# A two-level Strassen kernel for attention and four experts: seeding one product's PSUM bank from another, the second level for one more chunk, and a planner that takes what is due first

## The chip, the cores and the metric

One core of a Trainium2 chip runs the whole program. The metric is device time in microseconds (us) of one execution. Three executions of the kernel before took 1754.56, 1755.11 and 1755.19 us, so the median is 1755.11 us.

## What is computed

All data are float32. The first half is an attention without softmax, in 8 batches of 8 heads, 576 rows, 64 columns a head. Its result is laid out as 4608 tokens by 512 columns. The second half runs every token through 4 experts and adds the results with weights.

```python
kv  = einsum('bhsd,bhse->bhde', k, v)
out = einsum('bhsd,bhde->bhse', q, kv)
x   = out / sqrt(mean(out * out, -1) + 1e-6) * g_norm     # then (4608, 512)
p   = domain_probs / (domain_probs.sum(-1) + 1e-9)
for e in range(4):
    h    = maximum(x @ w1[e], 0)       # w1[e]: 512 x 1024
    out += p[:, e:e+1] * (h @ w2[e])   # w2[e]: 1024 x 512
```

## The kernel before

**Tiling.** The 4608 tokens are cut into 9 chunks of 512: chunk c of 0 to 7 has the first 512 rows of batch c, chunk 8 has the 64 rows left of each batch. For each expert e and each chunk c there is a step s = 9e + c, 36 in all, with an "up" part (x times w1) and a "down" part (h times w2). The step's down part runs beside the up part of the next step.

**Products.** Matrix products are done with Strassen's scheme (seven block products in place of eight, at the price of sums of blocks). `up` (L779) uses it twice: an outer loop over seven blocks m, and within each an inner loop over seven products mm in the order `ORDER = (1, 2, 6, 5, 7, 4, 3)` (L381), so 49 products a step. Each is two matmuls with 128 moving columns (L809). Only the first step is done plainly (`up_plain`, L878). The down part has two forms. `down` (L999) uses one level: seven products in two halves of tokens, each of four matmuls with 256 moving columns (L1017), 56 matmuls a step. `down_deep` (L1038) uses two levels: the seven outer blocks go in four groups, (1, 6), (7, 5), (4, 2) and (3), and for each group the seven inner products are made of 4 matmuls (2 in the last group) with 128 moving columns (L1090), 98 matmuls a step. The profile counts two records for each of these float32 matmuls. L1212 selects: `down_deep` for experts 1 to 3 and chunks 1 to 6, `down` for the rest.

**What an inner round does.** TensorE (PE) accumulates products 1, 6, 7, 4 of a round one after another in one PSUM bank (`u1` in `up`, `db` in `down_deep`), and the running sum is taken out after each by ScalarE (ACT): after 1, 6 and 7 into a buffer called `snap`, after 4 into its place in the result (L825, L1115). Product 2 has a bank of its own (`u2`, `ab`), and products 5 and 3 share a third. VectorE (DVE) adds a bank and a snap into the result (`total`, L833 and L1123): bank of 2 plus snap 1, bank of 5 plus snap 7, bank of 5 and 3 plus snap 6. There are two slots for each of the kinds `u1`, `u2`, `db` and `ab`[...]. In `up` the seven results are then added up (`combine`, L339, on DVE or on GpSimd, POOL), and a Relu on ACT (L792) gives h.

**What sets the order.** Nothing is ordered by hand. The class `Plan` (L34) holds every operation with a key (its place in the work), the engines that may do it and a cost. `layout` (L77) then walks through time: each free engine looks at its operations in order of key, up to a reach of 0.7 to 1.0 steps ahead, and takes the first one that is ready (its predecessors' ends plus 0.3 us across engines, 0.06 us on one), gives it its slots, and goes on. The result is a fixed order on each engine. A `port` operation on POOL also waits for the last such operation on DVE (L1234). Weights of the next expert are loaded during chunk 8 of the one before (L1201). The last step's result is written by SyncE (SP) with plain DMAs (L989), those of experts 1 to 3 otherwise by POOL with adding DMAs (L987).

Of the kernel before, what the change touches and what calls it, by code (L numbers as in the profile page):

```python
# [24 lines left out]
class Op:  # L25
    def __init__(self, key, cost, fn, reads, writes, kb, port):
        self.key, self.cost, self.fn, self.kb, self.port = key, cost, fn, kb, port
        self.outs = list(writes)
        self.bufs = list(dict.fromkeys(list(reads) + self.outs))
        self.deps = {}  # L30
        self.start = self.end = self.eng = None


class Plan:  # L34


# [9 lines left out]

    SPARE = {"big": 6, "small": 3}

    def __init__(self):
# [27 lines left out]
    def layout(self, slots, later, idle, idle_banks, idle_until):  # L77
# [14 lines left out]
        for e in todo:  # L92
            todo[e].sort(key=lambda o: (o.key, o.n))
        busy = {e: 0.0 for e in todo}
        bus = port = 0.0
# [27 lines left out]
        while left:  # L123
# [4 lines left out]
            for eng in todo:  # L128
# [5 lines left out]
                if not pending:  # L134
                    continue
                reach = pending[0].key + self.REACH[eng]
                for op in pending:
                    if op.key > reach:
                        break
                    if op.start is not None:  # L140
                        continue
                    when = ready(op, eng)
                    if when is None:
                        continue
                    if when > t:
                        heapq.heappush(wake, when)
                        continue
                    op.start, op.eng = t, eng
                    if eng == "SP":
# [35 lines left out]
                    moved = True  # L185
                    break
                if eng == "PE" and busy[eng] <= t and 1.6 <= t and front < idle_until:
# [26 lines left out]
def kernel(  # L214
# [9 lines left out]
    out: bass.AP,  # L224
):


# [152 lines left out]

    ORDER = (1, 2, 6, 5, 7, 4, 3)  # L381
    MERGED = (1, 6, 5, 7, 4, 3, 2)
# [396 lines left out]
    def up(s, e, views):  # L779
# [16 lines left out]
        for i, m in enumerate(OUTER):  # L796
            n = f"{s}_{m}"
            whole = made[m] = Buf("big", f"m{n}")
            bank = {1: Buf("u1", f"u1_{n}"), 2: Buf("u2", f"u2_{n}")}
            snap = {}  # L800
            for j, mm in enumerate(ORDER):
                key = s + (i + j / 7) / 7
                if mm == 5:
                    bank[2] = Buf("u2", f"u3_{n}")
                ps = bank[1 if mm in (1, 6, 7, 4) else 2]

                def product(eng, m=m, mm=mm, ps=ps):
                    for u in range(2):
                        nc.tensor.matmul(  # L809
                            ps.ap[:, u * P:(u + 1) * P],  # L810
                            lhsT=w1f[e][m][mm][1]()[:, u * P:(u + 1) * P], rhs=views[m][mm][1](),
                            start=(mm in (1, 2, 5) and u == 0), stop=True, skip_group_check=True,
                        )

                op = plan.add(
                    key, pe(2, P), product, reads=w1f[e][m][mm][0] + [views[m][mm][0]], writes=[ps],
                    after=last[-2:-1] if mm in (1, 2) else (),
                )
                if mm == 3:
                    last.append(op)  # L820

                def copy(to, where, ps=ps, key=key):
                    plan.add(
                        key - 0.4, act(HN),
                        lambda eng: nc.scalar.activation(  # L825
                            out=where(), in_=ps.ap[:, 0:HN], func=ACT.Copy),
                        reads=[ps], parts=[to],
                    )
# [8 lines left out]

                if mm in (1, 6, 7):
                    snap[mm] = Buf("snap", f"s{mm}_{n}")
                    copy(snap[mm], lambda b=snap[mm]: b.ap[:])  # L840
                if mm == 2:
                    total(0, 0, ps, snap[1])
                elif mm == 7:
                    total(1, 1, bank[2], snap[7])
                elif mm == 4:
                    copy(whole, lambda whole=whole: block(whole, 1, 0))
                elif mm == 3:
                    total(0, 1, ps, snap[6])
# [29 lines left out]
    def up_plain(s, e, c, key, span):  # L878
# [4 lines left out]
        for i in range(8):  # L883
            uh, a, u = i // 4, i // 2 % 2, i % 2
            bank = Buf("u1" if a == 0 else "u2", f"up{s}_{i}")
            for dh in range(2):
                w, low = corners[uh, dh]

                def product(eng, w=w, bank=bank, dh=dh, ut=2 * a + u):
# [6 lines left out]

                plan.add(
                    key + span * i / 8 - (1.1 if i < 4 and dh == 0 else 0.0), pe(2, NT), product,
                    reads=[w, low, xh[dh]], **({"parts": [bank]} if dh else {"writes": [bank]}),
                )  # L900
            for th, n in enumerate((1, 21) if uh == 0 else (2, 4)):
                plan.add(
# [96 lines left out]
    def down(s, e, c):  # L999
# [4 lines left out]
        for t in range(2):  # L1004
            banks = {}
            for j, m in enumerate(MERGED):
# [8 lines left out]
                def product(eng, m=m, t=t, ps=ps):  # L1015
# [10 lines left out]
                    after=second[-1:] if t and m in (1, 5) else (),  # L1026
                )
                if m == 2:
                    second.append(op)
# [8 lines left out]
    def down_deep(s, e, c):  # L1038
# [8 lines left out]
        for i, group in enumerate(((1, 6), (7, 5), (4, 2), (3,))):  # L1047
# [28 lines left out]
            outs = [pair] + [half[m] for m in group]  # L1076
            bank = {1: Buf("db", f"d1_{s}_{i}"), 2: Buf("ab", f"d2_{s}_{i}")}
            snap = {}
            for j, mm in enumerate(ORDER):
                key = at + n * j / 49  # L1080
                if mm == 5:
                    bank[2] = Buf("ab", f"d3_{s}_{i}")
                ps = bank[1 if mm in (1, 6, 7, 4) else 2]

                def product(eng, group=group, mm=mm, ps=ps, forms=forms):
                    for o, m in enumerate(group):
                        b, at = forms[m][mm]
                        for kt in range(2):
                            col = at * HN + kt * P
                            nc.tensor.matmul(  # L1090
                                ps.ap[:, o * P:(o + 1) * P], lhsT=b.ap[:, col:col + P],
                                rhs=w2q[e][m][mm][1]()[:, kt, :],
                                start=(mm in (1, 2, 5) and o == 0 and kt == 0), stop=(kt == 1),
                                skip_group_check=True,
                            )

                op = plan.add(
                    key, pe(2 * n, P), product,
                    reads=[b for m in group for b in (w2q[e][m][mm][0], forms[m][mm][0])],
                    writes=[ps], after=inner_last[-2:-1] if mm in (1, 2) else (),  # L1100
                )
                if mm == 3:
                    inner_last.append(op)
# [8 lines left out]
                def copy(where, key=key, ps=ps, n=n, group_of=group_of, **kw):  # L1112
                    plan.add(
                        key - 0.4, act(n * P),
# [14 lines left out]

                if mm in (1, 6, 7):  # L1130
                    snap[mm] = Buf("snap", f"ds{mm}_{s}_{i}")
                    copy(lambda b=snap[mm], g=group_of: g(b.ap), parts=[snap[mm]])
                if mm == 2:
                    total(0, 0, ps, snap[1])
                elif mm == 7:
                    total(1, 1, bank[2], snap[7])
                elif mm == 4:
# [57 lines left out]
    for e in range(E):  # L1195
        for c in range(NCH):
# [13 lines left out]
            if c == 1 and e:  # L1210
                inner[e]()
            if e and 1 <= c < NCH - 2:  # L1212
                down_deep(s, e, c)
# [9 lines left out]
    with tc.manual_schedule(engines={ENG.PE, ENG.DVE, ENG.Activation, ENG.Pool, ENG.SP}):  # L1223
# [4 lines left out]
        nc.vector.memset(bd_home[:], 0.0)  # L1228
        held = None
        for op in order:  # L1230
            made = op.fn(op.eng)
            if op.port and op.eng == "DVE":
# [33 lines left out]
```

## Time and profile before

The profiled execution took 1754.1 us; its span from the first to the last instruction is 1752.3 us, so 1.8 us lie around it. It is 1.0 us below the median of the three timed ones.

| engine | busy us | share of the span | instructions |
|---|---|---|---|
| PE, matmul | 1744.0 | 100% | 13970 |
| PE, weight load | 1659.0 | 95% | 13970 |
| DVE | 1119.1 | 64% | 1904 |
| POOL | 826.0 | 47% | 793 |
| ACT | 808.8 | 46% | 1897 |

PE's granted clock is 1.000. "Busy" for PE is a union of modelled, overlapping intervals: the mean of a matmul record (275 ns at 128 columns) is from its start to its modelled end, and the next starts long before that. What a matmul takes from PE is the distance between starts. A row such as `x8` in the timeline has eight records, and its first start and the next row's start give that distance.

### The profile page before, as it was taken

How to read it: one execution, taken by the hardware profiler on the slowest of the kernel's cores; microseconds unless marked ns; L12 is line 12 of the kernel's file. 1: busy time of each engine (PE TensorE's matmuls, PEld its weight loads, DVE VectorE, ACT ScalarE, POOL GpSimd, SP SyncE). 2: the span in 40 equal slices, each digit the busy share in tenths (PEclk: the TensorE clock that was granted, in tenths of full speed). 3: DMA queues.
4: the chain of work that ended last, by engine and by line, in shares of the span. 5: the costliest groups of instructions: out<-in, count | busy, mean ns of one | idle time of the engine just before them, and what ended most of it. 6: DMA issues, size and time to landing. Idle time of an engine off the chain costs nothing.

```text
span 1752.3 us, 35867 instructions
## 1 busy us (share of the span) xinstructions
PE 1744.0 (100%) x13970; PEld 1659.0 (95%) x13970; DVE 1119.1 (64%) x1904; ACT 808.8 (46%) x1897; POOL 826.0 (47%) x793
## 2 busy tenths in 40 slices
PE   9999999999999999999999999999999999999998
PEld 7799999999999999999999999999999999999997
DVE  4755554455674677777674577777674577777654
ACT  3454544454333445555543345555543445555541
POOL 2644553554345434444455534444455634444520
PEclk9999999999999999999999999999999999999999
DMA  9755544442443334444555434444465434444441
GB/s 236 242 160 161 167 128 136 151 140 85 148 153 103 106 100 110 109 109 109 136 154 133 108 95 110 108 111 107 111 169 136 117 98 108 111 108 111 109 109 37
DMA packets 148587, 220.78 MB, mean 126 GB/s; under 512 B 49601, under 2 KB 90817, under 8 KB 148417
## 3 DMA queue, kind: packets, MB, share of 16 engines
q1 hardware_dynamic: 133312, 191.21, 34.8%
q0 software_dynamic: 15104, 27.27, 11.0%
q8 instruction: 110, 1.80, 0.4%
q14 instruction: 61, 0.49, 0.1%
HBM read 145.30 MB, written 73.14 MB: 125 GB/s over the span
## 4 chain that ended last, share of the span: by engine, by line
PE 98%; SPq 1%; DMA 0%; POOL 0%; DVE 0%; issue 0%; ACT 0%
PE u L809 44%; PE db L1017 19%; PE db L1090 13%; PE ab L1090 10%; PE ab L1017 6%; PE u L891 2%; PE ab L602 1%; PE ab L584 1%; PE ab L612 1%; PE ab L569 1%; SPq L345 1%; DMA big<-in_v_dram 0%; PE ab L651 0%; POOL rt L521 0%; PE ab L666 0%; PE ab L636 0%
## 5 line engine op out<-in xcount | busy, mean ns | idle before, releaser
L833 DVE TENSOR_TENSOR big<-u,snap 128x256 f32<-128x256 f32 x696 | 290.6, 422 | 304.1 <-PE u L809 217.9
L809 PE MATMUL u<-xf,big 128*128 128x128 f32 x3248 | 453.9, 275 | 0.0
L825 ACT ACTIVATE snap<-u 128x256 f32<-128x256 f32 x735 | 281.7, 384 | 339.0 <-PE u L809 276.8
L339 DVE TENSOR_TENSOR big<-big,big 128x1024 f32<-128x1024 f32 (+1 forms) x354 | 410.6, 1175 | 32.9 <-ACT big L792 13.1
L809 PEld LDWEIGHTS u<-xf,big 128*128 128x128 f32 x3248 | 417.4, 192 | 7.3 <-issue 0.2
L809 PE MATMUL u<-xf,w1y 128*128 128x128 f32 x2652 | 371.6, 275 | 0.0
L809 PEld LDWEIGHTS u<-xf,w1y 128*128 128x128 f32 x2652 | 334.3, 192 | 2.0
L339 POOL TENSOR_TENSOR big<-big,big 128x256 f32<-128x256 f32 (+1 forms) x177 | 247.0, 1399 | 179.6 <-DVE big L339 67.2
L1017 PE MATMUL db<-big,big 128*128 128x256 f32 x1336 | 315.7, 380 | 0.0
L1017 PEld LDWEIGHTS db<-big,big 128*128 128x128 f32 x1336 | 241.6, 190 | 26.5
L792 ACT ACTIVATE big<-big 128x1024 f32<-128x1024 f32 x127 | 133.5, 1052 | 17.9 <-DVE big L339 12.4
L825 ACT ACTIVATE big<-u 128x256 f32<-128x256 f32 x232 | 89.0, 383 | 102.0 <-PE u L809 96.8
L987 POOL DMA_DIRECT2D out_dram<-big x110 | 100.3, 976 | 71.6 <-ACT big L964 53.0
L1115 ACT ACTIVATE snap<-db 128x256 f32<-128x256 f32 x216 | 76.6, 355 | 111.6 <-PE db L1090 100.8
L1123 DVE TENSOR_TENSOR big<-ab,snap 128x256 f32<-128x256 f32 (+1 forms) x204 | 79.0, 387 | 63.3 <-PE ab L1090 39.7
L339 POOL TENSOR_TENSOR big<-big 128x512 f32<-128x512 f32 (+1 forms) x75 | 89.6, 1200 | 63.0 <-DVE big L339 36.6
L964 ACT ACTIVATE big<-db,p_all 128x256 f32<-128x256 f32 x104 | 49.3, 474 | 141.0 <-PE db L1017 141.0
L1151 POOL TENSOR_TENSOR big<-big 128x512 f32<-128x512 f32 x19 | 24.1, 1269 | 164.4 <-DVE big L339 164.4
L971 DVE SCALAR_TENSOR_TENSOR big<-db,p_all,big 128x256 f32<-128x256 f32 x85 | 41.1, 483 | 86.4 <-PE db L1017 85.9
L1090 PE MATMUL db<-big,big 128*128 128x128 f32 x688 | 95.6, 275 | 0.0
L1090 PEld LDWEIGHTS db<-big,big 128*128 128x128 f32 x688 | 86.2, 192 | 0.1
L1017 PE MATMUL ab<-big,big 128*128 128x256 f32 x344 | 80.5, 379 | 0.0
(192 smaller groups left out, 2508.8 us busy)
## 6 DMA issues: line engine op xcount, KB each, us to landing
xf<-x SPq DMA_DIRECT2D x108, 512.0 KB, 3.5
out_dram<-big POOLq DMA_DIRECT2D x94, 256.0 KB, 5.3
xf<-x_h SPq DMA_DIRECT2D x81, 256.0 KB, 3.1
xf<-x SPq DMA_DIRECT2D x81, 256.0 KB, 3.3
x<-xf SPq DMA_DIRECT2D x36, 512.0 KB, 3.9
big<-in_moe_w_dram SPq DMA_DIRECT2D x28, 512.0 KB, 4.9
small<-in_q_dram SPq DMA_DIRECT2D x72, 128.0 KB, 3.7
kv<-in_k_dram SPq DMA_DIRECT2D x30, 288.0 KB, 3.4
```

The lines of the kernel that those rows point to most:

```text
L339: lambda eng: adder(eng).tensor_tensor(out=out_(), in0=a(), in1=b(), op=op),
L792: lambda eng: nc.scalar.activation(out=b.ap[:], in_=b.ap[:], func=ACT.Relu),
L809: nc.tensor.matmul(ps.ap[:, u * P:(u + 1) * P], lhsT=w1f[e][m][mm][1]()[:, u * P:(u + 1) * P], rhs=views[m][mm][1](), start=(mm in (1, 2, ...
L825: lambda eng: nc.scalar.activation(out=where(), in_=ps.ap[:, 0:HN], func=ACT.Copy),
L833: lambda eng: nc.vector.tensor_tensor(out=block(whole, a, t), in0=src.ap[:, 0:HN], in1=add_.ap[:], op=ALU.add),
L964: lambda eng: nc.scalar.activation(out=cell(i, half), in_=ap(), func=ACT.Copy, scale=prob()),
L971: lambda eng: nc.vector.scalar_tensor_tensor(out=cell(i, half), in0=ap(), scalar=prob(), in1=cell(i, half), op0=ALU.mult, op1=ALU.add,),
L987: nc.gpsimd.dma_start(out=dst, in_=cell(i)[parts, :], accum_op=ALU.add)
L1017: nc.tensor.matmul(ps.ap[:, 0:HN], lhsT=four(h[m])[:, kt // 2, t, kt % 2, :], rhs=w2f[e][m].ap[:, kt * HN:(kt + 1) * HN], start=(m in (1, ...
L1090: nc.tensor.matmul(ps.ap[:, o * P:(o + 1) * P], lhsT=b.ap[:, col:col + P], rhs=w2q[e][m][mm][1]()[:, kt, :], start=(mm in (1, 2, 5) and o ...
L1115: lambda eng: nc.scalar.activation(out=where(), in_=group_of(ps.ap), func=ACT.Copy),
L1123: lambda eng: nc.vector.tensor_tensor(out=cell(tq, dq), in0=group_of(src.ap), in1=group_of(add_.ap), op=ALU.add,),
```

## The change

Three things are changed.

**The seed.** After product 1, ACT copies the bank not into a snap but into the bank of product 2, and product 2 is added on top of it by PE (`start` is no longer set for it; it works on `parts` of the bank and reads it). What ACT then copies out is the finished block (0, 0), so DVE's `total(0, 0, ...)` is gone and a copy by ACT is there instead. The order of inner products becomes (1, 6, 2, 5, 7, 4, 3). Products 5 and 3 have their own buffer from the start of the round, and product 5 has to come after the copy that seeds (`after=seeds`). In `down_deep` the third bank of the last group is of kind `db`. An assertion while instructions are written out demands that PE's last product in the same slot was at least as wide as the seed.

**The second level for chunk 7.** L1212 becomes `c < NCH - 1`: steps 16, 25 and 34 are now done by `down_deep`.

**What is due first.** Each operation gets a due time: its key times 44 us (20 us later if PE isn't one of its engines), lowered where an operation that needs it is due earlier. ACT, DVE and POOL now take, of the operations within reach that are ready, the one with the earliest due time, in place of the first in order of key. PE and SP still take the first.

```diff
+        for op in self.ops:
+            op.due = op.key * self.STEP + (0.0 if "PE" in op.cost else self.LATE)
+        for op in reversed(self.ops):
+            for d in op.deps:
+                cross = self.SAME if op.cost.keys() == d.cost.keys() else self.CROSS
+                d.due = min(d.due, op.due - cross - min(d.cost.values()))
...
+                    if best is not None and op.due >= best.due:
                         continue
                     when = ready(op, eng)
...
+                    best = op
+                    if eng in ("PE", "SP"):
+                        break
...
-    ORDER = (1, 2, 6, 5, 7, 4, 3)
+    ORDER = (1, 6, 2, 5, 7, 4, 3)
...
-            bank = {1: Buf("u1", f"u1_{n}"), 2: Buf("u2", f"u2_{n}")}
+            bank = {
+                1: Buf("u1", f"u1_{n}"), 2: Buf("u2", f"u2_{n}"), 5: Buf("u2", f"u3_{n}"),
+            }
...
-                            start=(mm in (1, 2, 5) and u == 0), stop=True, skip_group_check=True,
+                            start=(mm in (1, 5) and u == 0), stop=True, skip_group_check=True,
...
-                    key, pe(2, P), product, reads=w1f[e][m][mm][0] + [views[m][mm][0]], writes=[ps],
-                    after=last[-2:-1] if mm in (1, 2) else (),
-                )
+                    key, pe(2, P), product,
+                    reads=w1f[e][m][mm][0] + [views[m][mm][0]] + ([ps] if mm == 2 else []),
+                    **{"parts" if mm == 2 else "writes": [ps]},
+                    after=last[-2:-1] if mm == 1 else seeds if mm == 5 else (),
+                )
...
-                if mm in (1, 6, 7):
+                if mm == 1:
+                    seeds = [copy(bank[2], lambda b=bank[2]: b.ap[:, 0:HN])]
+                elif mm in (6, 7):
                     snap[mm] = Buf("snap", f"s{mm}_{n}")
                     copy(snap[mm], lambda b=snap[mm]: b.ap[:])
                 if mm == 2:
-                    total(0, 0, ps, snap[1])
+                    copy(whole, lambda whole=whole: block(whole, 0, 0))
                 elif mm == 7:
-                    total(1, 1, bank[2], snap[7])
+                    total(1, 1, bank[5], snap[7])
...
-            if e and 1 <= c < NCH - 2:
+            if e and 1 <= c < NCH - 1:
                 down_deep(s, e, c)
```

`down_deep` has the same edits as `up`.

## The prediction

> **What bounds the kernel.** I read the page's totals first, then the chain that ended last, then PE's timeline for gaps, then the chain's end.
>
> ```profile
> PE 1744.0 (100%) x13970; PEld 1659.0 (95%) x13970; DVE 1119.1 (64%) x1904; ACT 808.8 (46%) x1897; POOL 826.0 (47%) x793
> ...
> PE 98%; SPq 1%; DMA 0%; POOL 0%; DVE 0%; issue 0%; ACT 0%
> PE u L809 44%; PE db L1017 19%; PE db L1090 13%; PE ab L1090 10%; PE ab L1017 6%; PE u L891 2%; PE ab L602 1%; PE ab L584 1%; PE ab L612 1%; PE ab L569 1%; SPq L345 1%; DMA big<-in_v_dram 0%; PE ab L651 0%; POOL rt L521 0%; PE ab L666 0%; PE ab L636 0%
> ```
>
> The chain is PE almost throughout: L809 (up), L1017 (plain down), L1090 (deep down). No other engine is busy over 64%. PE's timeline says what a matmul record takes, from start to start:
>
> ```profile
> 683.05 1.06 PE L1090 MATMUL db<-big,big 128*128 128x128 f32 x8
> 683.94 0.61 PE L809 MATMUL u<-xf,big 128*128 128x128 f32 x4
> 684.39 0.61 PE L809 MATMUL u<-xf,w1y 128*128 128x128 f32 x4
> 684.84 0.61 PE L1090 MATMUL ab<-x_rem,big 128*128 128x128 f32 x4
> 685.28 0.61 PE L1090 MATMUL ab<-kv,big 128*128 128x128 f32 x4
> 685.73 0.61 PE L809 MATMUL u<-xf,w1y 128*128 128x128 f32 x4
> ...
> 1723.26 8.80 PE L1017 MATMUL db<-big,big 128*128 128x256 f32 x40
> ...
> 1735.35 8.80 PE L1017 MATMUL ab<-big,big 128*128 128x256 f32 x40
> ```
>
> 683.05 to 685.73 is 24 records of 128 columns in 2.68 us: 0.1117 each. 1723.26 to 1735.35 is 56 records of 256 columns (40, and two rows of 8 left out) in 12.09 us: 0.2159 each. With such distances for every kind of record I went along PE's whole timeline. After about 80 us there is no gap over 0.2 us, and after about 450 us none at all. Up to 80 us PE loses 5.4 us in seven places, 2.6 of them on the first load of q. So nothing in the steady part can be won by shortening a wait: only PE work taken away counts, or waits brought in.
>
> **Part 1: the second level for chunk 7.** Three steps lose 56 matmuls of 256 columns and get 98 of 128. The order of the changed program's instructions confirms the counts (L1017's matmuls 1008 to 840, L1090's 1764 to 2058). Two records a matmul: 336 x 0.2159 = 72.5 us go, 588 x 0.1117 = 65.7 us come. Minus 6.9 us, all on the path.
>
> A rule speaks against this. The Trainium skill, "TensorE: Matmul & The Clock Gate", section "Back-to-back issue gap", gives about 81 ns a matmul at N = 128 in a real stream where weight loads count too, and 109.2 ns at N = 256 for the isolated gap (N/2.4 + 2.5). By that ratio, 0.74, the small record would cost 0.160 us, the new work 94.1 us, and the edit would lose 21.6 us. Here the ratio in the trace is 0.1117/0.2159 = 0.52, within rows where every record has its weight load (13970 of each). The row decides.
>
> What comes with it off PE: per step the deep form adds 21 subtractions and 7 sums on DVE or POOL and replaces 14 merges out of PSUM by 8 out of SBUF. The order has 1710 operations on DVE for 1902 and 753 on POOL for 788, so both are relieved over the program; ACT has 2273 for 1896. The next expert's weights are loaded in just that stage, and the deep form holds `big` buffers longer. I looked from which PE product each load is freed to the first product that reads its tile: the tightest w1 load has 47 us of PE work in between, 49 before. Landing takes 4.9 us (median) and two or three sums of 1.4 to 2.4 us follow. Cost nothing; it would begin to cost only if 35 us were eaten.
>
> **Part 2: the seed.** PE's products stay. Per round ACT has five copies for four, DVE two sums for three: 245 rounds in `up`, 84 in `down_deep`. DVE sheds 245 x 0.422 = 103 us there, which nobody waits for. The copy into PSUM has no row before. The nearest is L825, bank to snap, 384 ns. The skill's "ScalarE: Activation LUTs", section "Step-by-step: what each stage is for", holds that ScalarE writes faster to PSUM than to SBUF. By the rule it lies below 384 and by the row at 384; upwards I bound it at twice the row, 0.77. I take 0.38, the row it is nearest to.
>
> On ACT's queue the new copy stands in front of the snaps and Relus, and PE's product 6 and then 2 wait for it. How long a hand-over takes is seen where PE stalled:
>
> ```profile
> 73.42 0.60 PE L612 MATMUL ab<-ident,small 128*128 128x128 f32 x4
> 74.80 0.66 PE L569 MATMUL ab<-ident,small 128*128 128x128 f32 x4 [0.78 <-ACT big L618]
> ```
> ```profile
> 74.06 0.69 ACT L618 ACTIVATE big<-ab,gcol 128x512 f32<-128x512 f32 x1
> ```
>
> Four transposes of 0.109 end at 73.86. ACT starts 0.20 later, ends at 74.75, and PE goes on 0.05 later. So a copy of 256 columns needs 0.20 + 0.38 + 0.05 = 0.63 us from product to product on one bank, one of 128 columns (275 ns) 0.53. In the changed order I summed PE's work between two products on one bank. In `up`, after the start, four places have 0.89 us and the other 966 have 1.29 or more; before it was one at 0.89, which did not stall. In `down_deep` fifteen have 0.89, all in the last group with the short copy. At 0.77 for a copy the need is 1.02: 4 x 0.13 = 0.5 us. So the seed costs 0 if ACT is free. ACT is not always free:
>
> ```profile
> 664.70:708.50 43.80, 43.80 (x394) 43.80 (x394) 31.83 (x57) 22.98 (x56) 21.83 (x21) 1.00 0.43 107
> ```
>
> (Columns: window, length, then busy us of PE, weight load, DVE, ACT, POOL.) ACT gets 7 x 0.384 + 3 x 0.381 + 0.275 = 4.1 us more in a step: 27.1 of 43.8, 62%. That leaves room; a Relu of 1.05 us in front of a copy makes 1.7 us, and can stall a place of 1.29 by 0.4. Before, such places existed in the same number (301 products that wait 1.3 us behind ACT, 288 after) and none stalled. I take 0, and 2 us as the upper end.
>
> **Part 3: what is due first.** It moves work on ACT, DVE and POOL only; what it costs shows at the two ends.
>
> At the start, product 6 now comes 0.39 us after product 1 (it was two products later): needs 0.63, costs 0.25. One transpose that stalled 0.5 us on DVE has one product less in front of it: up to 0.45 more. The three 1024-wide sums that DVE now does first (3 x 1.22 us) delay forms that lay ready by 30 us and are needed at about 60: free. I take +0.5, between -1.5 (most of the waits of 0.54, 0.94 and 0.50 us near 70 us go) and +1.5.
>
> At the end, the last down part needs h2, the last sum of `up`, and then h3. Before:
>
> ```profile
> 1720.65 0.42 DVE L833 TENSOR_TENSOR big<-u,snap 128x256 f32<-128x256 f32 x1
> 1720.98 2.35 DVE L339 TENSOR_TENSOR big<-big,big 128x1024 f32<-128x1024 f32 x2
> ...
> 1723.37 1.06 ACT L792 ACTIVATE big<-big 128x1024 f32<-128x1024 f32 x1 [1.16 <-DVE big L339]
> ...
> 1724.81 2.68 POOL L339 TENSOR_TENSOR big<-big,big 128x1024 f32<-128x1024 f32 x1
> ```
>
> h3 was ready at 1727.5; PE asked for it three products after 1723.26, at 1728.4. In the changed order h2 goes to POOL, behind a port wait on a DVE sum (L1151) of the deep step that now fills this stage. From the last product of `up`: 0.20 to DVE, 0.42 + 0.29 + 0.78 for three DVE operations, 0.38 to POOL (as ACT to POOL above), 2.5 (between the 2.37 of L339's mean and 2.68), 0.1 and 1.05 for Relu, 0.1 and 1.23 for h3 on DVE, 0.05: 7.1 us. PE has two deep pairs and three plain products until then: 0.45 + 0.45 + 3 x 1.727 = 6.1 us. A stall of 1.0, between 0.3 and 2. Two hand-overs with 0.45 us of cover (need 0.53) just ahead disappear in it. The last store keeps its place: eight DMAs after the last merge.
>
> **The sum.** -6.9 + 0 + 0.5 + 1.0 = -5.4 us. Against the profiled execution: 1754.1 - 5.4 = 1748.7. The median is 1.0 above that execution: 1749.7.
>
> **The rivals.**
>
> *More is won.* The new choice also clears the startup waits and the tail isn't late: -6.9 - 1.5 + 0.3 = -8.1, so 1747.0. For it: 2.0 us of startup waits are behind ACT or DVE. Against: the same pairs stand next to each other in the new order (the 0.94 wait has still no work in front of it).
>
> *The gain is largely given back.* ACT at 62% meets Relu and copy at once more often than before: 2 us in the middle, 2 at the end, 1.5 at the start. 1755.1 - 6.9 + 5.5 = 1753.7, no change that counts. Against: no stall in 1300 us before.
>
> *Slower: the seed is late.* PE stands for each seed until ACT has done it. With c the time of a copy, its time in the queue included, PE loses c + 0.25 less the work in front. Summed over the changed order's places: 0.7 + 3.1 us at c = 0.8, 1.5 + 6.3 at 1.0, 5.6 + 9.4 at 1.1. It decides from c of about 1.0, where it eats the 6.9; at 1.1 the time is 1755.1 - 5.4 + 15 = 1764.7. For it: ACT is in order, and DVE's sum waited for nothing of the kind. Against: c would have to be 2.6 times the nearest row.
>
> *It doesn't do what it says.* If PE overwrote the seed rather than adding, instructions and waits would be the same, and so the time: no case of its own.
>
> **Chances and range.** Forecast 1749.7: 0.67. More won: 0.13. Given back: 0.15. Slower: 0.05. A measurement of this kernel tells about 0.2%, 3.5 us, from no change. The first two are faster by more: 0.80; the third is the same: 0.15; the last slower: 0.05. The range goes from 1746.8, just past the second case, to 1753.2, short of the third's 1753.7, which has all three uncertain ends (start, middle, tail) at their worst at once. About 0.85 lies within.
>
> **What would show it.** Right: L1017 with 1680 records and the 128-column kinds with 588 more, at unchanged distances; no PE gap between 100 and 1690 us; a seed row on ACT near 0.38; one PE wait of about 1 us near the end, behind h3. Wrong: PE waits on ACT at products 6 or 2 in the middle; a seed row over 0.8; another distance of the 128-column records; PE waiting on weights near 900 or 1300 us.

## The result, and the profile after

The changed kernel takes 1748.39 us (median; 1746.86 to 1748.91) against 1754.84 for the kernel before (four executions by now): ratio 0.9962, 95% interval 0.9945 to 0.9979, 6.5 us less. The forecast was 1749.7. The profiled execution took 1748.91 us with a span of 1747.1, 5.2 less than the profiled one before, where 5.4 had been worked out. How close these two come is luck, as the stretches below show.

The page's totals, and its chain by engine:

```profile
PE 1738.6 (100%) x14222; PEld 1664.1 (95%) x14222; DVE 1151.4 (66%) x1712; ACT 931.6 (53%) x2274; POOL 719.7 (41%) x758
...
PE 99%; DMA 0%; DVE 0%; ACT 0%; SPq 0%; issue 0%; ACTq 0%
```

PE has 252 records more, 588 less 336, and yet ends earlier. ACT is busy 123 us longer, POOL 106 us less. DVE has 192 operations fewer and yet is busy 32 us longer, since it now does more of the wide sums that either engine may do (`combine`, 429 against 354 in the largest group). The chain is PE still. What a record costs is read from PE's timeline, as before:

```profile
682.97 0.61 PE L1119 MATMUL db<-big,small 128*128 128x128 f32 x4
683.41 1.06 PE L830 MATMUL u<-xf,big 128*128 128x128 f32 x8
684.31 0.61 PE L1119 MATMUL ab<-x_rem,big 128*128 128x128 f32 x4
684.75 0.61 PE L1119 MATMUL ab<-kv,big 128*128 128x128 f32 x4
685.20 0.61 PE L830 MATMUL u<-xf,big 128*128 128x128 f32 x4
685.65 1.06 PE L830 MATMUL u<-xf,w1y 128*128 128x128 f32 x8
686.54 0.61 PE L830 MATMUL u<-xf,big 128*128 128x128 f32 x4
...
1730.18 5.34 PE L1044 MATMUL ab<-big,big 128*128 128x256 f32 x24
1735.37 1.89 PE L1044 MATMUL ab<-big,small 128*128 128x256 f32 x8
1737.09 1.89 PE L1044 MATMUL ab<-small,big 128*128 128x256 f32 x8
1738.82 3.62 PE L1044 MATMUL ab<-big,big 128*128 128x256 f32 x16
```

(L830 is `up`, L1119 `down_deep`, L1044 `down`; before they were L809, L1090, L1017.) 682.97 to 686.54 is 32 records in 3.57 us: 0.1116 each. 1730.18 to 1738.82 is 40 in 8.64: 0.2160. The distances are those of before, so the exchange gives its 6.9 us in full.

For every kernel here I cut PE's time in two: its records times their distances ("work"), and all that lies between ("gaps"), by stretch of the span. A kernel's gaps carry the same small error of the distances everywhere, so only differences count.

| us | work | gaps, first 30 us | 30-100 | 100-450 | 450-1700 | after 1700 |
|---|---|---|---|---|---|---|
| before | 1730.4 | 3.7 | 4.6 | 7.8 | -0.4 | 0.0 |
| after | 1723.5 | 5.6 | 4.2 | 7.1 | -0.4 | 0.9 |

Work -6.9, the first 30 us +1.9, the rest of the start and the first expert -1.1, the tail +0.9: -5.2, the whole difference of the two spans.

The tail, from the timeline of all engines (rows of the last hidden blocks and of PE):

```profile
1717.74 5.34 PE L1044 MATMUL db<-big,big 128*128 128x256 f32 x24
1718.41 2.36 POOL L360 TENSOR_TENSOR big<-big,big 128x1024 f32<-128x1024 f32 x1 [0.72 <-DVE big L1185]
1720.81 1.06 ACT L813 ACTIVATE big<-big 128x1024 f32<-128x1024 f32 x1 [1.37 <-POOL big L360]
1721.89 1.23 DVE L360 TENSOR_TENSOR small<-big,big 128x1024 f32<-128x1024 f32 x1
1723.17 1.99 PE L1044 MATMUL db<-big,small 128*128 128x256 f32 x8
```

h2 on POOL behind DVE's sum, Relu on ACT, h3 on DVE, then PE. 24 records of 0.2159 from 1717.74 end at 1722.92; PE goes on at 1723.17, 0.25 us later. With 0.34 us ahead of it, at a hand-over, and PE's restarts the tail costs 0.9.

In the first 30 us the transfers fill the DMA engines (the windows' view of the changed kernel; columns as in the prediction, then granted clock, share of the DMA engines and GB/s):

```profile
1.00:30.00 29.00, 27.58 (x251) 24.25 (x252) 6.30 (x9) 9.49 (x20) 8.27 (x10) 1.00 1.02 235
```

Most of the +1.9 there is PE's own pace. Its timeline before, and then after:

```profile
5.94 0.63 PE L569 MATMUL ab<-ident,small 128*128 128x128 f32 x4 [0.49 <-DMA small<-in_q_dram]
6.41 2.13 PE L1219 MATMUL ab<-ident 128*128 128x128 f32 x18
8.56 0.92 PE L584 MATMUL ab<-kv,kv 96*64 96x64 f32 x24
...
6.52 1.08 PE L590 MATMUL ab<-ident,small 128*128 128x128 f32 x4 [1.07 <-DMA small<-in_q_dram]
7.39 3.43 PE L1253 MATMUL ab<-ident 128*128 128x128 f32 x18
10.76 0.92 PE L605 MATMUL ab<-kv,kv 96*64 96x64 f32 x24
```

The load of q lands 0.6 us later, and the same 22 records then take 4.24 us (6.52 to 10.76) for 2.62: PE goes at about half its pace up to 10.1 us, and in the profile before only up to 5.4. (The clock column of the row above shows 1.00 all the same.) That is 2.2 us; a wait of 0.4 for v, near 20 us, is gone. Across the 14 profiles of this study, PE's gaps in the first 30 us lie between 3.7 and 5.6 us, and the two highest are the two with a half pace up to 10 us. tail_dve below, whose start is the changed kernel's, has 3.8. So the +1.9 is scatter of the execution, and not the change. Why the half pace lasts longer in some executions is not shown.

### The profile page after: what moved, and what is told of

The parts are those of the page before. It is cut to its first block, busy times and chain, and to the rows that moved or that the text cites. A ratio compares the mean times of both kernels' runs of the same rounds, so it can differ in the third digit from the quotient of the medians.

```text
span 1747.1 us, 36218 instructions
## 1 busy us (share of the span) xinstructions
PE 1738.6 (100%) x14222; PEld 1664.1 (95%) x14222; DVE 1151.4 (66%) x1712; ACT 931.6 (53%) x2274; POOL 719.7 (41%) x758
## 4 chain that ended last, share of the span: by engine, by line
PE 99%; DMA 0%; DVE 0%; ACT 0%; SPq 0%; issue 0%; ACTq 0%
PE u L830 44%; PE db L1044 17%; PE db L1119 16%; PE ab L1119 10%; PE ab L1044 4%; PE u L917 2%; PE ab L605 2%; PE ab L623 1%; PE ab L590 1%; PE ab L633 1%; PE ab L1253 1%; PE ab L672 0%; DMA small<-in_q_dram 0%; PE db L623 0%; PE ab L687 0%; PE ab L657 0%
## 5 line engine op out<-in xcount | busy, mean ns | idle before, releaser
L360 DVE TENSOR_TENSOR big<-big,big 128x1024 f32<-128x1024 f32 (+1 forms) x429 | 479.1, 1128 | 61.9 <-ACT big L813 33.4
L830 PE MATMUL u<-xf,big 128*128 128x128 f32 x3536 | 508.4, 275 | 0.0
L830 PEld LDWEIGHTS u<-xf,big 128*128 128x128 f32 x3536 | 455.5, 192 | 4.8 <-issue 0.9
L830 PE MATMUL u<-xf,w1y 128*128 128x128 f32 x2652 | 381.3, 275 | 0.0
L857 DVE TENSOR_TENSOR big<-u,snap 128x256 f32<-128x256 f32 x446 | 188.1, 422 | 254.6 <-PE u L830 170.9
L830 PEld LDWEIGHTS u<-xf,w1y 128*128 128x128 f32 x2652 | 342.8, 192 | 3.9
L849 ACT ACTIVATE snap<-u 128x256 f32<-128x256 f32 x490 | 187.9, 383 | 249.0 <-PE u L830 211.5
L1044 PE MATMUL db<-big,big 128*128 128x256 f32 x1192 | 280.2, 380 | 0.0
L1044 PEld LDWEIGHTS db<-big,big 128*128 128x128 f32 x1192 | 216.3, 190 | 24.5 <-issue 0.2
L849 ACT ACTIVATE big<-u 128x256 f32<-128x256 f32 x446 | 170.0, 383 | 95.7 <-PE u L830 63.0
L360 POOL TENSOR_TENSOR big<-big,big 128x256 f32<-128x256 f32 (+1 forms) x116 | 139.4, 1217 | 111.6 <-DVE big L360 75.1
L1119 PE MATMUL db<-big,big 128*128 128x128 f32 x788 | 113.0, 275 | 0.0
L1147 ACT ACTIVATE snap<-db 128x256 f32<-128x256 f32 (+1 forms) x168 | 60.0, 357 | 94.5 <-PE db L1119 87.2
L849 ACT ACTIVATE u<-u 128x256 f32<-128x256 f32 x245 | 91.0, 372 | 25.9 <-PE u L830 10.2
L1119 PEld LDWEIGHTS db<-big,big 128*128 128x128 f32 x788 | 100.3, 192 | 0.0
L1119 PE MATMUL db<-kv,big 128*128 128x128 f32 x624 | 88.6, 275 | 0.0
L1119 PE MATMUL ab<-kv,big 128*128 128x128 f32 x588 | 84.1, 275 | 0.0
```

What stands on the lines that cost most here:

```text
L360: lambda eng: adder(eng).tensor_tensor(out=out_(), in0=a(), in1=b(), op=op),
L830: nc.tensor.matmul(ps.ap[:, u * P:(u + 1) * P], lhsT=w1f[e][m][mm][1]()[:, u * P:(u + 1) * P], rhs=views[m][mm][1](), start=(mm in (1, 5) ...
L849: lambda eng: nc.scalar.activation(out=where(), in_=ps.ap[:, 0:HN], func=ACT.Copy),
L857: lambda eng: nc.vector.tensor_tensor(out=block(whole, a, t), in0=src.ap[:, 0:HN], in1=add_.ap[:], op=ALU.add),
L1044: nc.tensor.matmul(ps.ap[:, 0:HN], lhsT=four(h[m])[:, kt // 2, t, kt % 2, :], rhs=w2f[e][m].ap[:, kt * HN:(kt + 1) * HN], start=(m in (1, ...
L1119: nc.tensor.matmul(ps.ap[:, o * P:(o + 1) * P], lhsT=b.ap[:, col:col + P], rhs=w2q[e][m][mm][1]()[:, kt, :], start=(mm in (1, 5) and o == ...
```

## The experiments

Theory: PE's work is the gain, -6.9; seed and choice only keep or spend some of it in waits. Rivals: the seed or the choice wins or costs as much on its own; the tail or ACT's queue holds back more than 1 us. Times of the runs are medians; the ratio is to the kernel before in the same job. "Net" is PE's work and gaps without the first 30 us, as a difference to before.

**Chunk 7 alone** (deep7_alone), on the kernel before:

```diff
-            if e and 1 <= c < NCH - 2:
+            if e and 1 <= c < NCH - 1:
```

> The kernel before with only the second level for chunk 7 (three steps); no seed, no due times. My theory (only PE work counts): 336 records of 256 columns go and 588 of 128 come, so minus 6.9 us, less what its own tail loses (0 to 1 us): 5.9 to 6.9 us faster than before, with L1090's records still 0.1117 us apart and no PE gap between 450 us and the last step. Rival A (most of the gain comes from the seed and the due times): within 2 us of before. Rival B (small matmuls are limited by their weight loads): slower by up to 20 us.

1751.39 us, ratio 0.9977 [0.9968, 0.9987]; net -4.2. The work is 1723.5, as in the changed kernel. But it has waits of its own: 0.7 us near 930 and 0.7 near 1330, at the two expert changes, and 1.2 at the tail. So it gains 3.6 us, and not the 5.9 to 6.9 of the theory, which allowed for no waits at the expert changes; rivals A and B are out. The exchange alone is 60% of the gain. With the other two parts the waits at the expert changes are gone, the tail costs 0.9, and the start and the first expert give the rest.

**Seed and choice without chunk 7** (no_deep7), on the changed kernel:

```diff
-            if e and 1 <= c < NCH - 1:
+            if e and 1 <= c < NCH - 2:
```

> The changed kernel with chunk 7 done by one level as before; seed and due times stay. My theory: PE's work is that of before, so the time is that of before, plus or minus 1 us (start and tail), and PE shows no gap between 450 us and the last step. Rival A (seed and due times bring the gain): 3 to 6 us faster than before. Rival C (ACT with 62% of a step costs PE waits that something else hid): slower than before by 2 us or more.

1756.39 us, 1.0008 [0.9999, 1.0016]; net +2.5. PE's work is that of before, and two new waits of 1.8 and 1.6 us stand at 891 and 1294, where the theory had no gap. Rival C's size is met in the trace, but not by its cause: PE waits for DVE. The first, in the timeline's rows of DVE and PE:

```profile
889.92 1.23 DVE L360 TENSOR_TENSOR big<-big,big 128x1024 f32<-128x1024 f32 x1 [2.99 <-DMA big<-in_moe_w_dram]
...
892.54 0.42 DVE L857 TENSOR_TENSOR big<-u,snap 128x256 f32<-128x256 f32 x1
...
893.01 0.71 PE L830 MATMUL u<-xf,w1y 128*128 128x128 f32 x4 [1.62 <-DVE big L857]
```

A sum of the next expert's weights stands at the head of DVE's queue for 2.99 us, until its load lands. The total that frees PE's bank is queued behind it. The three loads of weights issued from 870 to 900 us took:

```profile
DMA to landing us min/median/max: 3.5/4.9/11.6
```

The 11.6 is the load in question (issued at 878.18, landed at 889.83). Four writes of results were issued within 3.5 us of it and took 8.4 to 11.2.

PE itself does not need these weights for another 40 us. What hurts is the place of the sum in DVE's queue, together with a late load.

**The same with that sum due later** (no_deep7_late), on no_deep7; all sums of the next expert's w1 get the later key:

```diff
-                weights_1(e + 1, s + 0.0, 0.12, s + 0.3)()
+                weights_1(e + 1, s + 0.0, 0.12, s + 0.5)()
```

> The kernel with seed and due-first choice but without chunk 7's second level (1756.4 when it ran), with the first-level sums of the next expert's w1 given a due time 0.2 step later. Theory: the PE waits of 1.8 us near 891 and 1.6 near 1294 came of one such sum, which stood at the head of DVE's queue for 3.0 and 2.8 us until its load landed, with the totals that free PSUM behind it. Then both waits go, gaps fall from 18.2 to about 15, and the time by 3 us, to 1752.5 to 1754.5. Rival: DVE is simply overfull there, and another operation takes the place: waits of over 1 us in the same two places stay, time 1755.5 to 1757.

1755.30 us, 1.0002 [0.9994, 1.0010]; net -1.1, so 3.6 us below the run above in the trace. Both waits are gone:

```profile
887.49 1.22 DVE L360 TENSOR_TENSOR big<-big,big 128x1024 f32<-128x1024 f32 x1
...
890.10 0.42 DVE L857 TENSOR_TENSOR big<-u,snap 128x256 f32<-128x256 f32 x1
...
891.42 1.06 PE L830 MATMUL u<-xf,w1y 128*128 128x128 f32 x8
```

But the edit did not do this by moving the sum. From 540 to 893 us DVE does the same kinds of operations in the same order in both runs, and again ahead of the second wait: the sum of the run above stands in the same place (887.49), with the same operations between it and the total. It does not wait because its load has landed, at 887.06. The weights' loads of that stretch here:

```profile
DMA to landing us min/median/max: 3.5/5.2/8.2
```

8.2 us in place of 11.6, among the same four writes of results; near 1290 us it is 9.6 in place of 11.5. So the two traces together show that the wait comes and goes with the landing of one load. Whether a later due time would remove it was not tested, as this edit left the order there as it was. Why the load was faster, and whether the edit has a part in that, is open. The time lies between the two expectations; the medians differ by only 1.1 us, less than the 3 expected, and the intervals overlap.

**The seed alone** (seed_alone), on the kernel before; the edit is the diff above without the second level and with the choice by key:

```diff
+                    best = op
+                    break
```

> The kernel before with only the seed; the first ready operation in order of key is taken as before, and chunk 7 has one level. My theory: 245 + 84 copies move to ACT and as many sums leave DVE, nobody waits: within 1.5 us of before, the copy from bank to bank at 0.37 us. Rival C: PE waits on ACT at products 6 and 2, 2 us or more slower.

1759.09 us, 1.0022 [1.0015, 1.0029]; net +2.5. The theory is missed. The size is that of rival C, but the waits are not on ACT. The work is unchanged; two gaps of 0.2 to 0.3 us come up in each of four steps of the first expert (100 to 450 us: 9.3 for 7.8), all of them behind DVE, and one of 0.8 us at 894. One of the small ones:

```profile
196.24 0.61 PE L829 MATMUL u<-big,big 128*128 128x128 f32 x4
...
196.48 0.41 DVE L856 TENSOR_TENSOR big<-u,snap 128x256 f32<-128x256 f32 x1
...
196.94 0.71 PE L829 MATMUL u<-big,w1y 128*128 128x128 f32 x4
```

Four records end at 196.69; PE goes on at 196.94, just after DVE's total has emptied the bank (196.89). The one at 894 is of the kind seen in no_deep7, a sum of weights that waits for its load:

```profile
892.29 1.23 DVE L359 TENSOR_TENSOR big<-big,big 128x1024 f32<-128x1024 f32 x1 [1.68 <-DMA big<-in_moe_w_dram]
...
895.37 0.71 PE L829 MATMUL u<-xf,w1y 128*128 128x128 f32 x4 [0.66 <-DVE big L856]
```

By itself the seed is a loss that can be measured; some 0.9 of the 2.5 us hang on that one load.

**The choice alone** (due_alone), on the kernel before; the edit is the first block of the diff:

```diff
+                    best = op
+                    if eng in ("PE", "SP"):
+                        break
```

> The kernel before with only the choice of what is due first. My theory: the steady part has no PE gap to win, so only start and tail can move: within 1.5 us of before. Rival A: 3 us or more faster, with the waits near 70 us gone.

1754.23 us, 0.9996 [0.9987, 1.0004]; net -1.2, all of it in the first 450 us. Not to be told from no change.

**Choice and chunk 7 without the seed** (due_deep7), the changed kernel with this taken back (main lines; the banks and `down_deep` likewise):

```diff
-    ORDER = (1, 6, 2, 5, 7, 4, 3)
+    ORDER = (1, 2, 6, 5, 7, 4, 3)
...
-                            start=(mm in (1, 5) and u == 0), stop=True, skip_group_check=True,
+                            start=(mm in (1, 2, 5) and u == 0), stop=True, skip_group_check=True,
...
-                    copy(whole, lambda whole=whole: block(whole, 0, 0))
+                    total(0, 0, ps, snap[1])
```

> The changed kernel without the seed: chunk 7's second level and the choice by due time stay, the first block's total is a DVE sum again. My theory, that the seed was worth nothing on PE's path: PE's records are the same 14222 in number, work 1723.5 us, gaps 15 to 18 us (those of before, and a tail of about 1), so 1747.5 to 1749.5 us, ratio to before 0.996, the same as the changed kernel within 0.2%. Rival A, that the seed is needed because DVE, with 245 more sums in its queue, comes late beside the new deep steps: PE waits on DVE at the expert changes (near 890 to 980 and 1290 to 1380 us), 3 us or more slower than the changed kernel, 1751.5 or over. Rival B, that the seed costs (the seed alone was 4 us slower than before): 1744 to 1746.

1749.87 us, 0.9974 [0.9964, 0.9984]; net -5.1, 1.9 more than the changed kernel. It has 0.35 us at each of 930 and 1329, where PE waits for a snap of ACT, and 2.0 at the tail: 0.7 behind a snap of ACT, 0.5 behind h3, and the last 0.8 behind a merge on DVE:

```profile
1733.44 1.00 DVE L985 SCALAR_TENSOR_TENSOR big<-ab,p_all,big 128x256 f32<-128x256 f32 x2 [2.97 <-PE ab L1031]
...
1733.98 2.21 PE L1031 MATMUL ab<-big,big 128*128 128x256 f32 x9 [0.58 <-DVE big L985]
```

DVE was idle for 2.97 us before that merge and waited for PE: the two banks were handed over with too little work between, and DVE's queue was not full. So in company the seed wins about 1.9 us in the trace, but no wait here shows that it does so by relieving DVE. The times agree in sign, 1749.87 for 1748.39, but their intervals overlap: within 0.2% of each other, and just above the range that my theory gave. Rival A named the place of the small waits, but neither their size nor the engine; rival B is out.

**Seed and chunk 7, choice by key** (by_key), on the changed kernel:

```diff
-                    if eng in ("PE", "SP"):
-                        break
+                    break
```

> The changed kernel with the choice by key again, as before: seed and chunk 7 stay, only the choice by due time is undone. My theory, that the three parts add: seed alone cost 4 us (waits of 0.2 to 0.3 us in the first expert and one near 894 us), chunk 7 alone won 3.5, so 1754 to 1756, 6 to 8 us slower than the changed kernel, with PE waits of 0.2 us at product 6 in the first 440 us. Rival, that the seed alone was slow for the expert change only, which chunk 7's second level reshapes: 1748 to 1750, within 0.2% of the changed kernel. Either way PE's work is 1723.5 us; the difference is in gaps.

1752.05 us, 0.9985 [0.9978, 0.9991]; net -2.3, 4.8 more than the changed kernel. The time lies between the two expectations. But 1.6 of the 4.8 us are not the choice. From 77 to 81 us PE goes at half its pace (the window's granted clock is 0.57), and eight records that take 1.73 us elsewhere take 3.19, to 80.99:

```profile
77.00:81.00 4.00, 4.00 (x15) 3.13 (x14) 4.00 (x14) 1.22 (x4) 2.98 (x1) 0.57 0.04 16
...
77.80 3.27 PE L1043 MATMUL db<-big,big 128*128 128x256 f32 x8
80.99 0.92 PE L604 MATMUL ab<-kv,kv 96*64 96x64 f32 x24
```

No other profile here has that. Without it 3.2 us are left: 0.4 before 100 us, 2.2 up to 450 us (9.3 for 7.1, the small waits of the seed alone) and 0.6 at the expert changes; the wait at 894 is not there. In most of them PE waits for DVE, as here, and not for a copy that seeds:

```profile
76.20 0.43 PE L686 MATMUL ab<-ident,small 64*128 64x64 f32 x4 [1.04 <-DVE small L548]
```

**ACT under load** (seed_x3): the changed kernel with the copy that seeds in `up` made three times over (`copy` repeats its instruction `times` times), with the same result.

```diff
-                    seeds = [copy(bank[2], lambda b=bank[2]: b.ap[:, 0:HN])]
+                    seeds = [copy(bank[2], lambda b=bank[2]: b.ap[:, 0:HN], times=3)]
```

> The changed kernel with the seeding copy of the up part made three times over (the same order on every engine, 490 copies more on ACT, the same result): from 0.37 to about 1.1 us from the first copy's start to the last one's end. My theory (what counts is the PE work between products 1 and 6): 27 of 245 places have less in front than the 1.35 us needed then, and lose 2.8 us together; with the snaps delayed behind it some more: 3 to 8 us slower than the changed kernel. Rival (ACT is nearly the bound, and any more on it goes to PE): 490 x 0.37 = 181 us more on ACT show as tens of us.

1759.96 us, 1.0029 [1.0018, 1.0041]; 11.6 us over the changed kernel, 10.9 of it in PE's gaps. Both expectations are missed, mine from below: the waits on the seed are at 22 places, where I had counted 27, but they lose 6.4 us by themselves and not 2.8. The row of ACT's group, and a place where PE waits for it:

```profile
L849 ACT ACTIVATE u<-u 128x256 f32<-128x256 f32 x735 | 271.3, 369 | 41.0 <-PE u L830 9.5
```
```profile
750.26 1.16 ACT L849 ACTIVATE u<-u 128x256 f32<-128x256 f32 x3
750.66 0.61 PE L830 MATMUL u<-xf,w1y 128*128 128x128 f32 x4
...
751.47 0.71 PE L830 MATMUL u<-xf,w1y 128*128 128x128 f32 x4 [0.21 <-ACT u L849]
```

490 copies of 0.37 us are 181 us of ACT's time and cost PE 10.9. At 0.37 for a seed ACT's queue has room, at 1.16 it has not. That is the "slower" rival's mechanism made to happen: it put 5.6 us on `up` at 1.1 us a copy, and it needed three times the true copy.

**The tail on DVE** (tail_dve), on the changed kernel (the same for h3):

```diff
-                add(key, unit(2), made[1], made[4])
+                add(key, unit(2), made[1], made[4], where=dve if s == E * NCH - 1 else either)
```

> The changed kernel with h2 and h3 of the last step bound to DVE. In the changed kernel PE loses about 0.9 us after 1716 us: 0.34 and 0.09 at two hand-overs with 0.45 us of work in front, then 0.25 before the product with h3, the rest in restarts of 0.1. My theory (POOL's 2.4 us sum behind a port wait is what makes h3 late): the wait before h3 goes, the two hand-overs stay, 0.3 to 0.5 us faster than the changed kernel in PE's last record. Rival (h3 is late because of the Relu on ACT behind four merges, not of POOL): no change of that wait.

1748.52 us, 0.9962 [0.9949, 0.9974]. The tail's gaps go from 0.9 to 0.5 us, the 0.25 before h3 gone. Too little to be seen in the time.

**The second level for chunk 8 of experts 1 and 2** (deep8), and **both** (deep8_tail), on the changed kernel:

```diff
-            if e and 1 <= c < NCH - 1:
+            if e and c and s < E * NCH - 1:
```

> The changed kernel with the second level also for chunk 8 of experts 1 and 2 (two more steps). My theory: 2 x (112 x 0.2159 - 196 x 0.1117) = 4.6 us less PE work, and the next expert's first weight load keeps tens of us of cover: 4.6 us faster than the changed kernel. Rival (the deep form's buffers hold up the weights of the next expert there): PE waits on weights after 950 and 1350 us, no gain.

> Both: the second level for chunk 8 of experts 1 and 2, and h2 and h3 of the last step on DVE. My theory: 4.6 + 0.4 = 5.0 us faster than the changed kernel, about 1743.5 us if that one is at 1748.5, and 11 us faster than before.

1748.30 us, 0.9965 [0.9951, 0.9979], and 1749.09, 0.9967 [0.9954, 0.9979]. Two more steps bring another -4.5 us of work (1719.0), but 5.3 us of gaps come up at the expert changes, 2.6 in each, and neither expectation of a gain is met. The largest in the 900s:

```profile
971.99 1.05 ACT L813 ACTIVATE big<-big 128x1024 f32<-128x1024 f32 x1
...
972.93 1.69 ACT L991 ACTIVATE big<-big,p_all 128x256 f32<-128x256 f32 x4
...
974.53 0.36 ACT L849 ACTIVATE snap<-u 128x256 f32<-128x256 f32 x1
...
974.95 0.71 PE L830 MATMUL u<-xf,big 128*128 128x128 f32 x4 [1.49 <-ACT snap L849]
```

A Relu and four merges stand in front of the snap that frees PE's bank. That is 1.75 us of the 2.6; the other 0.85, at 937, is a hand-over to DVE and back with no work in front. No wait is for weights, which was the rival. So two thirds of the loss are in ACT's queue, as the second rival of the prediction said of the change itself; the tail's 0.4 us does not help.

**The tail on DVE, without the seed** (due_deep7_tail); the two edits shown above together.

> The kernel without the seed, and with the last step's h2 and h3 on DVE. Expected 0 to 0.7 us below the run without the seed: its tail wait of 0.3 to 1 us gets shorter, the rest stays. Rival, that without the seed DVE has 84 more sums of the deep form there and h2 comes later than from POOL: 0.5 us slower.

1750.89 us, 0.9977 [0.9968, 0.9986]. The tail goes from 2.0 to 1.5 us, but this execution has 5.6 us of gaps in the first 30, as against 4.1, with the half pace up to 10 us that the changed kernel's profile has. No gain shows.

**Taken together.** Net by the trace, and the time by the ratio (of 1754.8 us), as differences to before:

| parts | net us | by the ratio |
|---|---|---|
| choice | -1.2 | -0.7 |
| seed | +2.5 | +3.9 |
| chunk 7 | -4.2 | -4.0 |
| seed, choice | +2.5 | +1.4 |
| seed, chunk 7 | -2.3 | -2.6 |
| choice, chunk 7 | -5.1 | -4.6 |
| all three | -7.1 | -6.7 |

The two columns agree within 1.5 us, so to that measure PE's work and gaps account for the times; differences between parts of 1 or 2 us are no better known than that. (Without the half pace at 77 us, seed and chunk 7 would have -3.9 in the first column.) No other version that was run is faster than the changed kernel by more than the noise.

## Why the prediction was right

*Part 1, -6.9.* Exact: 252 records more at unchanged distances, work 1730.4 to 1723.5. The loss of 21.6 us that the prediction set against it took its two figures from different cases: in the Trainium skill's "TensorE: Matmul & The Clock Gate", "Back-to-back issue gap", 81 ns at N = 128 is for a stream, and 109.2 ns at N = 256 for a single matmul. The page's formula for the single matmul at both widths gives an estimate of 55.8/109.2 = 0.51, and the rows agree with that ratio (0.52); the stream's extra time at N = 128 does not show in them. The row of 0.1117 us decided, and chunk 8's two steps, which brought another 4.5 us of work, confirm it.

*The cover of the weights, 0.* Right for the changed kernel, which has no wait near 900 or 1300 us. The reasoning was incomplete: it asked how far PE is from needing the weights, and not what is queued on DVE behind the first sum that needs the load. That is where no_deep7 lost 3.4 us. And "both are relieved" holds for POOL only: DVE has fewer operations, but is busy for 1151.4 us where it was 1119.1.

*Part 2, 0.* The size of the copy was right:

```profile
L849 ACT ACTIVATE snap<-u 128x256 f32<-128x256 f32 x490 | 187.9, 383 | 249.0 <-PE u L830 211.5 <-DVE big L857 22.6 <-DVE big L1155 3.8
...
L849 ACT ACTIVATE u<-u 128x256 f32<-128x256 f32 x245 | 91.0, 372 | 25.9 <-PE u L830 10.2
```

372 ns against 383 into a snap. The skill's rule ("ScalarE: Activation LUTs", the section named in the prediction) points the right way, by 11 ns. As a part, the seed isn't 0: it is +2.5 alone and -1.9 in company. Without it the changed kernel has 0.9 us more at the expert changes and 1.1 more at the tail. "Nobody waits" for what DVE sheds is not refuted by that, since none of those waits is shown to be DVE's queue; what failed is to price the seed by itself, when it changes the order of the whole.

*Part 3, start +0.5.* Measured -0.3 from 30 to 100 us. The waits of 0.54 and 0.94 near 70 us stayed, the one of 0.50 went, where up to 0.45 more had been feared, and one of 0.20 came at product 6 behind the seed, where 0.25 had been worked out. The first expert's -0.7 was not foreseen: before, I had called gaps of under 0.2 us none. Nor were the 2.6 us that the prediction put on the first load of q all waiting: 0.5 is the wait, and the rest PE's half pace in the 18 records ahead of it (4.10 us). The part as a whole was mis-assigned. I gave it +1.5, start and tail; taken back, it costs 3.2 in the trace, most of it in waits for DVE up to 450 us. The sum came right although the parts' terms did not: with the start's scatter of +1.9, which no term had, the spans differ by 5.2, and without it by 7.1.

*Part 3, tail +1.0.* Measured 0.9. The chain is the one that was worked out, h2 on POOL and h3 on DVE, but the wait before h3 is 0.25 and not 1.0. The rest is the two hand-overs just ahead, which were to disappear in it, and restarts. That the number fits is luck.

*The rivals.* The measured -6.5 lies between the forecast's -5.4 and the -8.1 of "more won", but not by that mechanism: the startup waits stayed. "Given back" did not come here, and did in deep8. "Slower" needed a copy of about 1 us; it was 0.37.

The sum without the first 30 us: -6.9 - 0.3 - 0.7 + 0.9 = -7.0, where -5.4 was forecast. The terms that were mis-sized are the start (by 0.8) and the first expert (by 0.7); the tail's is right in its sum and not in its place. The time itself moved by -6.5.

## What to carry to other kernels

Where one engine is the whole chain, price an edit by that engine's records and their measured distances first; then look for waits in the new order as a whole, since edits to one plan don't add (the seed was +2.5 alone, -1.9 in company). Check the engine's pace before a gap is called a wait: in three of the profiles here 1.6 us of "gap" were records at half speed. For a load, ask not only when its user is due, but what stands behind its first reader in an in-order queue. When a further exchange of the same kind brings less than its work (deep8: 4.5 us of work, nothing in the time), look for the engine that empties the banks, and see what it does just before.

## What the hardware showed that was not expected

One load of weights took 11.6 us to landing in no_deep7, with four writes of results issued within 3.5 us of it, where the median of that stretch is 4.9; in no_deep7_late, at the same place with the same neighbours, it took 8.2. The first 30 us, with the DMA engines full (share 1.02), cost PE 3.7 to 5.6 us in gaps, more scatter than most single edits here are worth. PE went at half its pace up to 4.4 to 6.6 us in twelve of the profiles and up to 10 us in two, and in by_key once more for 3.4 us at 77 us, with a granted clock of 0.57 for the window. What sets that in these executions is not shown. And ACT's copy from bank to bank is hardly faster than from bank to SBUF: 372 ns for 383.
